# The first p moved ahead of the first k on SyncE's queue, and every operation in a newly searched order: a packed-attention and token-mixing kernel on one Trainium2 core

## The chip, the cores and the metric

The kernel runs on one core of a Trainium2 chip. The metric is the device time of one execution in microseconds. Before the change the median of three runs is 122.78 us (122.41 to 123.39). A measurement of this kernel can tell a difference of about one per cent from none.

## What is computed

All inputs are fp32; there are 8 batches (index b), 8 heads, 576 tokens, 64 channels a head and 32 packed queries a head (p).

```python
def sm_attn(qq, kk, vv):                       # softmax attention, scale 1/8
    s = scale * qq @ kk.T
    a = exp(s - max(s)); a = a / sum(a)
    return a @ vv
p_packed = sm_attn(p, k, v)                    # 32 x 64 for each batch and head
attn     = sm_attn(q, p_packed, p_packed)      # 576 x 64 for each batch and head
x = attn, heads side by side                   # 8 x 576 x 512
W = (x @ w_q) @ (x @ w_k).T / 8                # 576 x 576 for each batch
out = relu(W @ x) @ w_out                      # 8 x 576 x 512, fp32
```

## The kernel before

Nothing is scheduled by a compiler. The kernel defines about a hundred small operations, and a long string, `SCHEDULE`, lists every instance of them in the order in which they are recorded. Each engine works through its own instructions in exactly that order, so an instruction that waits holds up everything behind it on its engine, and engines wait for each other by semaphores only. An item reads `name@b`, then a letter and, after a colon, the PSUM banks: `kt0@1:3` is operation `kt0` of batch 1 into bank 3. The letter `s`, `v` or `g` puts a copy on ScalarE (ACT), VectorE (DVE) or GpSimd (POOL); `f` or `c` runs a matrix product on TensorE (PE) as one 128-column or as two 64-column matmuls.

What happens to a batch, with the lines under which the profile lists it:

- `LK LQ LV` (L148) load k, q, v of a batch by POOL's DMA queue, which converts to bf16 on the way. Eight of POOL's transfers can be under way; the issue of a further one first waits for the landing of the one eight places before it.
- `kt0 kt1`, `qt0 qt1` (L304) transpose k and q on PE; `ke0 ke1 qe0 qe1` copy the results from PSUM to SBUF (copies are L135 on ACT, L137, L139 and L141 on DVE).
- `s0` (L345) multiplies p by k, `nm0` (L355, DVE) takes the negative row maximum, `ex0 ex1` (L359, ACT) the exponentials and their sums, `rc1` the reciprocals, `rm` (L408, POOL) a masked copy of these.
- `xt0 xt1` (L376) transpose the weights, `xe0 xe1` copy them, `pv` (L421) multiplies by v, `pp` (L430) scales: this is p_packed. `pt pte` transpose it.
- `e0 e1 e2` (L470, L482) are the scores of q against p_packed; `mx0..2` and `sb0..2` (L498, L502, DVE) take and subtract maxima, `x0` (L531, ACT) is the exponential, `sm0` the sums (one reduction on DVE, L537, or a tree of five adds on POOL, L540 to L543), `rr0` the reciprocals, `ml0 ml1 ml2` (L551, DVE or POOL) the products that give the attention weights in three parts. `at0 at1` (L571, L574) transpose them, `ae0 ae1` copy.
- `pq wk wz wq g y m0 m1 m2` (L449, L628, L639, L660, L675, L683, L699, L714, L739) are the mixing products without ever forming x; `r00..r11 r2` apply the relu in the copy out of PSUM.
- `o0..o4` (L755) are the projections by `w_out`, `oe0..oe4` copy them, `st0..st2` and `sc0..sc3` (L786, L782, L772) store by SyncE's (SP's) DMA queue.

The batches overlap: while one is in its projections, the next ones are in their softmaxes and the loads run two to three batches ahead. Items `w1@..`, `w2@..` (L203) are one or two dummy products with a tile of zeros, which keep PE running where the order expects it to have nothing to do.

The first batch has a way of its own. Its k comes unconverted by SP's queue in two halves, `KA` and `KB` (L169, tile `k_f`); `cA0 cA1 cB0 cB1` convert them (tile `k_sb`), `kf0..kf3` transpose on PE (L257; `kf0`, `kf1` of the half of `KA`, `kf2`, `kf3` of that of `KB`), `kfe0..kfe3` copy. Its p comes fp32 by SP's queue (`PF`, L166, tile `p_f`); `pfc` converts it (tile `p_h`), `tp` transposes (L219), `lp` copies it into `pT_bd`. The p of the other batches comes by POOL's queue (`PB`, L179, tile `p_b`), is transposed by 32 matmuls `tr` (L233) and copied by `lq0`, `lq1`. The small weights are loaded by `cw0..cw3` (L278) and `wo0`, `wo1` (L287). `id` makes the identity on POOL.

The tiles of each name rotate through the buffers that `SLOTS` gives (six each for k, q and v, for example).

Of the kernel before, what the change touches and what calls it, by code (L numbers as in the profile page):

```python
# [21 lines left out]
    kt0@3:7 xe0@2s kt1@3:5 g@0f:2 LV@3 LK@5 rm@2 sb0@1 pv@2:3 LK@6 wqe@0s ke1@3v ke0@3s ge@0s y@0:5
    x0@1 pp@2 s0@3:0 ye@0s m0@0:45 r00@0s r01@0s nm0@3 m1@0:67 ex0@3 r11@0v w1@0c:3 qt1@2:3 qe1@2v
    pt@2f:5 pte@2v ex1@3 qt0@2:7 qe0@2v r10@0s w1@0f:3 sm0@1g rr0@1 ml1@1v ml0@1g ml2@1g LQ@5
    xt1@3c:0 xe1@3s LQ@4 LV@4 kt0@4:1 e0@2c:7 mx0@2 LK@7 xt0@3c:5 xe0@3v rc1@3 ke0@4s kt1@4:2 ke1@4s
    rm@3 e2@2:0 LQ@6 mx2@2 e1@2f:6 mx1@2 at0@1f:1 at1@1f:4 sb2@2 o1@0f:5 ae0@1s sb0@2 s0@4:0 sb1@2
    ae1@1s wk@1f:4 nm0@4 wq@1:7 wqe@1v oe1@0s x0@2 o0@0c:6 oe0@0v ex0@4 ex1@4 qt0@3:5 wz@1 o2@0f:7
    xt0@4f:6 wkx@1 wke@1s sm0@2v xe0@4v rr0@2 qe0@3s xt1@4f:0 g@1f:2 ge@1s pv@3:3 pp@3 y@1:5 ye@1s
    oe2@0s qt1@3:1 xe1@4v pt@3c:3 LV@5 m0@1:05 qe1@3v m1@1:46 m2@1f:7 ml1@2g ml0@2g pq@2:1 r00@1v
    pqe@2v pte@3s pq@3:2 e0@3f:3 r01@1s e2@3:0 pqe@3v e1@3f:5 r11@1s r2@1s r10@1s mx2@3 mx1@3 sb1@3  # L30
    sb2@3 ml2@2g LV@6 mx0@3 at0@2c:6 kt1@5:1 kt0@5:4 ae0@2s ke1@5s at1@2f:7 o2@1f:5 ae1@2s o3@0f:6
    wk@2f:7 wz@2 rc1@4 sb0@3 ke0@5v s0@5:0 oe2@1v wkx@2 x0@3 kt1@6:3 kt0@6:5 wke@2s oe3@0s wq@2:6
    nm0@5 ke0@6s ex1@5 ke1@6v wqe@2v o1@1f:7 g@2f:3 ex0@5 ge@2s qt1@5:4 qt0@5:6 st1@0 oe1@1v qt0@4:7
    y@2:2 sm0@3g rr0@3 qe1@5v qt1@4:0 ye@2v m1@2:23 qe0@4v r11@2v ml0@3g rm@4 qe0@5s o4@1f:6 qe1@4s
    rc1@5 r10@2s pv@4:4 m0@2:01 ml1@3g oe4@1s r00@2s ml2@3v at0@3f:7 xt1@5f:2 pp@4 ae0@3s r01@2v
    pt@4f:3 rm@5 LQ@7 pte@4v at1@3f:4 ae1@3s xt0@5f:0 xe1@5v e0@4f:3 mx0@4 LV@7 xe0@5s e1@4f:7 mx1@4
    o3@2f:5 oe3@2s sb0@4 wk@3f:2 e2@4:1 mx2@4 wz@3 wkx@3 wke@3s wq@3:6 wqe@3s kt0@7:0 s0@6:3 sb2@4
    o2@2c:1 sb1@4 kt1@7:6 ke0@7s x0@4 o0@1f:2 pq@4:0 nm0@6 ex1@6 ke1@7v ex0@6 sm0@4g oe2@2v oe0@1s
    qt1@6:6 pqe@4v qt0@6:1 qe0@6s qe1@6v rc1@6 s0@7:3 g@3f:2 ge@3s nm0@7 rm@6 pv@5:6 y@3:0 pp@5
    o3@1f:2 ye@3v rr0@4 ex1@7 ex0@7 pt@5f:7 xt0@6f:6 pte@5v xt1@6f:0 xe0@6v ml1@4g st0@1 m2@3f:1  # L40
    r2@3s e1@5f:7 e0@5f:3 ml0@4g oe3@1s m1@3:64 r10@3s xe1@6v pv@6:0 ml2@4g pq@5:2 o1@2c:5 pqe@5s
    mx1@5 mx0@5 pp@6 r11@3s sb1@5 e2@5:2 pt@6c:0 pte@6s at0@4f:1 mx2@5 rc1@7 ae0@4s at1@4f:4 sb0@5
    xt0@7f:7 rm@7 sb2@5 xe0@7s e1@6f:0 ae1@4v xt1@7f:3 xe1@7v st0@0 o4@3f:2 mx1@6 sb1@6 x0@5 sm0@5g
    wk@4f:3 m0@3:76 r01@3v wq@4:1 oe4@3s e2@6:4 wz@4 wke@4v wkx@4 oe1@2s r00@3s e0@6c:0 mx0@6 st2@3
    wqe@4s o0@2c:2 oe0@2s qt1@7:6 g@4c:1 o0@3c:5 st1@2 qe1@7s sb0@6 ge@4v y@4:2 mx2@6 pv@7:0 st2@1
    rr0@5 ml0@5g sb2@6 pp@7 qt0@7:7 ye@4s m1@4:43 oe0@3s ml2@5v m0@4:01 x0@6 pt@7c:5 pq@6:2 qe0@7v
    o2@3c:6 at0@5c:7 st1@1 pte@7s ml1@5g st0@2 r00@4v pqe@6v e0@7c:0 e2@7:5 r11@4s at1@5c:3 pq@7:2
    r01@4v ae0@5v mx0@7 r10@4s o1@4c:1 e1@7c:7 sm0@6g oe2@3s ae1@5s mx2@7 wk@5c:3 sb0@7 o0@4c:4 wz@5
    mx1@7 sb2@7 wq@5:0 o3@3c:5 sb1@7 oe1@4s rr0@6 wkx@5 wqe@5v o1@3c:7 wke@5s oe0@4s st0@4 x0@7
    ml1@6g pqe@7v oe3@3s st1@3 g@5c:3 ge@5s o2@4c:2 oe1@3s y@5:3 ml0@6g ye@5s ml2@6v sm0@7v rr0@7  # L50
# [782 lines left out]
```

## Time and profile before

| | before |
|---|---|
| median of 3 runs | 122.78 us (122.41 to 123.39) |
| the profiled execution | 122.19 us, its span 120.4 us |
| busy: PE, PE's weight loads, DVE, ACT, POOL | 105.2, 69.2, 94.0, 88.6, 59.5 us |
| moved by POOL's queue | 14.49 MB in 13,920 packets |
| moved by SP's queue | 10.68 MB in 3,984 packets |
| granted TensorE clock | 1.00 throughout |

The span goes from the first to the last instruction on the core; the 1.8 us between it and the execution's own time lie around it. Busy time on PE is that of matmuls whose ends are modelled. A row of the timeline gives start, length, engine, line, operation, output and inputs, and in brackets how long the engine had been idle before it and what ended that. A row of a group by form gives count, busy time and mean in ns, and the idle time before. A row of a transfer gives the time from issue to landing.

### The profile page before, as it was taken

How to read it: one execution, taken by the hardware profiler on the slowest of the kernel's cores; microseconds unless marked ns; L12 is line 12 of the kernel's file. 1: busy time of each engine (PE TensorE's matmuls, PEld its weight loads, DVE VectorE, ACT ScalarE, POOL GpSimd, SP SyncE). 2: the span in 40 equal slices, each digit the busy share in tenths (PEclk: the TensorE clock that was granted, in tenths of full speed). 3: DMA queues.
4: the chain of work that ended last, by engine and by line, in shares of the span. 5: the costliest groups of instructions: out<-in, count | busy, mean ns of one | idle time of the engine just before them, and what ended most of it. 6: DMA issues, size and time to landing. Idle time of an engine off the chain costs nothing.

```text
span 120.4 us, 4740 instructions
## 1 busy us (share of the span) xinstructions
PE 105.2 (87%) x2041; PEld 69.2 (57%) x2055; DVE 94.0 (78%) x192; ACT 88.6 (74%) x159; POOL 59.5 (49%) x85
## 2 busy tenths in 40 slices
PE   6955677879998999999999989999999969999980
...
DMA  3999999999999999999999999994940484045793
GB/s 51 372 207 204 207 205 208 194 208 208 208 208 204 209 206 210 207 209 207 209 289 208 208 213 203 290 251 155 393 178 5 195 328 169 14 186 201 310 383 145
DMA packets 17925, 25.47 MB, mean 212 GB/s; under 512 B 2160, under 2 KB 14448, under 8 KB 17904
## 3 DMA queue, kind: packets, MB, share of 16 engines
q0 software_dynamic: 13920, 14.49, 71.6%
q1 hardware_dynamic: 3984, 10.68, 23.5%
...
## 4 chain that ended last, share of the span: by engine, by line
PE 45%; ACT 16%; DVE 14%; DMA 14%; POOL 4%; issue 3%; SPq 1%; DVEq 0%; POOLq 0%
PE psum L755 16%; DMA out_dram<-o_sb 8%; DMA p_f<-in_p_dram 6%; PE psum L304 5%; ACT e1T L359 4%; ACT e L531 4%; DVE mx L498 3%; PE psum L571 3%; DVE e L502 3%; PE psum L421 3%; ACT kT L135 3%; PE psum L714 2%; PE psum L660 2%; PE psum L345 2%; PE psum L203 2%
## 5 line engine op out<-in xcount | busy, mean ns | idle before, releaser
L755 PE MATMUL psum<-w_out,r 128*64 128x512 bf16 (+1 forms) x184 | 30.7, 380 | 0.7 <-issue 0.5
L551 POOL TENSOR_TENSOR a<-e,rr 128x512 bf16<-128x512 f32 (+1 forms) x16 | 16.0, 1019 | 10.4 <-DVE rr L547 7.3
L135 ACT ACTIVATE o_sb<-psum 128x512 f32<-128x512 f32 x25 | 14.9, 602 | 6.0 <-PE psum L755 4.1
L755 PEld LDWEIGHTS <-r 128*64 128x64 bf16 (+1 forms) x192 | 12.4, 106 | 11.1 <-issue 1.3
L359 ACT ACTIVATE e1T<-psum,nmax 128x576 bf16<-128x576 f32 x16 | 11.7, 739 | 5.0 <-DVE nmax L355 4.9
L135 ACT ACTIVATE kT<-psum 128x1280 bf16<-128x1280 bf16 (+2 forms) x10 | 10.4, 1043 | 5.1 <-DVE mx L498 3.3
L498 DVE TENSOR_REDUCE mx<-psum 128x16 f32<-128x512 f32 (+1 forms) x24 | 12.7, 550 | 0.9 <-PE psum L470 0.8
L540 POOL TENSOR_TENSOR rt<-e 128x576 f32<-128x576 f32 x5 | 7.1, 1417 | 12.4 <-ACT e L531 12.3
L502 DVE TENSOR_TENSOR e<-psum,mx 128x512 f32<-128x512 f32 (+1 forms) x24 | 12.6, 548 | 0.1
L355 DVE TENSOR_REDUCE nmax<-psum 128x2 f32<-128x1152 f32 x8 | 10.8, 1355 | 2.0 <-PE psum L345 1.8
L203 PE MATMUL psum<-zero 128*64 128x512 bf16 (+1 forms) x45 | 10.7, 477 | 1.4 <-DVE zero L182 1.2
L135 ACT ACTIVATE r<-psum 128x512 bf16<-128x512 f32 x19 | 10.8, 600 | 1.0 <-PE psum L714 1.0
L304 PE MATMUL psum<-ident,q_sb 128*64 128x128 bf16 x288 | 10.6, 220 | 0.6 <-DVE r L137 0.3
L531 ACT ACTIVATE e<-e 128x1152 f32<-128x1152 f32 x8 | 9.4, 1169 | 1.2 <-DVE e L502 1.2
L304 PEld LDWEIGHTS <-q_sb 128*64 128x64 bf16 x288 | 9.1, 110 | 1.7 <-issue 0.5
L137 DVE TENSOR_SCALAR r<-psum 128x512 bf16<-128x512 f32 x13 | 8.6, 684 | 0.9 <-PE psum L714 0.8
L304 PE MATMUL psum<-ident,k_sb 128*64 128x128 bf16 x252 | 8.6, 219 | 0.0
L135 ACT ACTIVATE qT<-psum 128x1280 bf16<-128x1280 bf16 (+1 forms) x7 | 8.1, 1152 | 0.6 <-PE psum L304 0.6
L542 POOL TENSOR_TENSOR rt<-rt 128x288 f32<-128x288 f32 (+2 forms) x15 | 7.9, 528 | 1.2
L304 PEld LDWEIGHTS <-k_sb 128*64 128x64 bf16 x252 | 7.8, 110 | 0.9 <-issue 0.2
L135 ACT ACTIVATE a2T<-psum 128x768 bf16<-128x768 bf16 (+1 forms) x12 | 8.1, 702 | 0.2
L408 POOL TENSOR_TENSOR rm<-mask,rrec 128x256 f32<-128x256 f32 x8 | 5.0, 627 | 6.2 <-DVE rrec L369 6.2
...
## 6 DMA issues: line engine op xcount, KB each, us to landing
...
q_sb<-in_q_dram POOLq DMA_DIRECT2D x8, 576.0 KB, 14.8
v_sb<-in_v_dram POOLq DMA_DIRECT2D x8, 576.0 KB, 17.2
k_sb<-in_k_dram POOLq DMA_DIRECT2D x7, 576.0 KB, 17.3
k_f<-in_k_dram SPq DMA_DIRECT2D x2, 576.0 KB, 4.5
out_dram<-ox SPq DMA_DIRECT2D x4, 256.0 KB, 2.7
out_dram<-o_sb SPq DMA_DIRECT2D x4, 256.0 KB, 2.5
w_out<-in_moe_w_out_dram POOLq DMA_DIRECT2D x2, 256.0 KB, 11.9
```

Source lines behind the costliest of these rows:

```text
L135: nc.scalar.activation(dst, src, func, scale=scale)
L137: nc.vector.tensor_scalar(dst, src, 0.0, None, op0=MAX)
L203: nc.tensor.matmul(bank(ks[0])[r], zero[:, r], zero, start=True, stop=True, skip_group_check=True,)
L304: nc.tensor.transpose(tp[64 * g2:64 * g2 + 64, gp, :, 64 * (j - j0):64 * (j - j0) + 64], S_[b][src][:, gp + 2 * g2, order[j]], ident,)
L355: nc.vector.tensor_reduce(tile("nmax", [P, 2], fp32, b), S_[b]["s1"], axis=AX, op=MAX, negate=True)
L359: nc.scalar.activation(tile("e1T", [P, NJ, 2, 64], bf16, b)[:, :, h2], S_[b]["s1"][:, h2].rearrange("a (j s) -> a j s", j=NJ), EXP, bias=S ...
L498: nc.vector.tensor_reduce(units(i, tile("mx", [P, NU, 1], fp32, b)), S_[b]["e", i], axis=AX, op=MAX)
L502: nc.vector.tensor_tensor(units(i, tile("e2", [P, NU, L], fp32, b)), S_[b]["e", i], m.to_broadcast((P, m.shape[1], L)), op=SUB,)
L531: nc.scalar.activation(e, e, EXP, scale=scale)
L542: nc.gpsimd.tensor_tensor(t[:, :, 0:w], t[:, :, 0:w], t[:, :, w:2 * w], op=ADD)
L551: (nc.gpsimd if on == "g" else nc.vector).tensor_tensor(tile("a2", [P, NU, L], bf16, b)[:, r], S_[b]["e2"][:, r], S_[b]["rr"][:, r].to_bro ...
L755: nc.tensor.matmul(ps[r], src[:, i, r], w_out[:, i, :], start=(i == 0), stop=(i == 3),)
```

## The change

`PF` stands in front of both k halves on SP's queue, the half of `KB` comes before that of `KA`, `PB` is the first transfer on POOL's queue, and the items of the string stand in a new order, with new banks, new letters for some copies and products, and the dummy products elsewhere. Every operation on every batch is still there once; only the number of dummy products differs (30 before, 28 after). The functions and `SLOTS` are unchanged. The k, q and v loads after the first batch keep their order among each other.

```diff
 SCHEDULE = """
-    w1@0c:1 KA@0 LQ@0 cA0@0s w1@0c:0 cA1@0v w1@0f:1 w2@0c:1 w1@0c:0 KB@0 PB@0 w2@0c:1 w1@0c:0 LV@0
-    cw3@0 id@0 kf0@0:1 cB1@0v cB0@0v LK@1 w1@0f:5 PF@0 pfc@0v LQ@1 kfe0@0s kf1@0:4 kfe1@0v kf2@0:0
-    kfe2@0s kf3@0:2 w1@0c:1 tp@0:5 kfe3@0v lp@0v s0@0:0 nm0@0 qt1@0:3 LK@2 w1@0f:5 ex1@0 ex0@0
-    tr@0:57 w1@0c:6 qe1@0s lq0@0v rc1@0 xt0@0f:2 xe0@0v w1@0c:1 xt1@0c:5 cw2@0 xe1@0v qt0@0:1 qe0@0v
-    lq1@0s w1@0c:0 cw0@0 cw1@0 pv@0:4 rm@0 pp@0 pt@0c:5 pte@0v w1@0f:2 w1@0f:6 e1@0c:5 mx1@0 e0@0f:2
-    e2@0:6 w1@0c:4 LV@1 mx0@0 mx2@0 kt1@1:0 ke1@1s sb0@0 LK@3 kt0@1:3 ke0@1v sb1@0 sb2@0 LV@2 s0@1:0
-    nm0@1 x0@0 sm0@0v rr0@0 w1@0c:4 qt1@1:6 qe1@1s w1@0c:3 w1@0f:3 ex0@1 qt0@1:4 w1@0f:3 LQ@2
-    kt1@2:5 ml0@0v kt0@2:7 ml1@0g ex1@1 rc1@1 xt1@1f:0 at0@0f:2 ke1@2s xt0@1f:1 xe0@1s ke0@2v ml2@0v
-    s0@2:5 at1@0f:3 rm@1 ae0@0v qe0@1v LK@4 nm0@2 pq@0:2 xe1@1s pv@1:0 ae1@0s w1@0c:4 pqe@0s wk@0f:2
...
+    w1@0c:2 PF@0 w1@0c:0 PB@0 LQ@0 LV@0 id@0 w1@0f:1 KB@0 cB1@0v w1@0c:0 w2@0f:2 pfc@0s w1@0f:1
+    w1@0f:5 LK@1 LQ@1 w2@0f:1 KA@0 cA1@0v tp@0:0 w1@0c:2 w2@0f:1 kf3@0:5 cB0@0s kf2@0:2 w1@0c:1 LK@2
+    tr@0:34 lp@0s kfe2@0v w1@0f:1 kf1@0:6 cA0@0s kf0@0:1 w1@0c:2 kfe1@0v kfe0@0v kfe3@0s s0@0:0
+    nm0@0 cw0@0 w1@0f:5 w1@0f:5 lq0@0s cw2@0 ex0@0 lq1@0v w1@0c:6 w1@0f:6 w1@0c:5 w1@0c:3 ex1@0
+    rc1@0 cw3@0 qt0@0:6 xt1@0f:0 rm@0 xt0@0f:1 xe0@0v qt1@0:2 LV@1 xe1@0s qe1@0v pv@0:0 pp@0 w1@0f:3
+    qe0@0s pt@0c:2 pte@0v e0@0c:0 mx0@0 sb0@0 w1@0c:6 kt0@1:5 e2@0:7 mx2@0 sb2@0 kt1@1:2 cw1@0
+    ke0@1s e1@0f:6 mx1@0 sb1@0 ke1@1s w1@0f:0 x0@0 LK@3 LV@2 s0@1:3 nm0@1 ex1@1 ex0@1 qt1@1:6
+    w1@0f:2 LQ@2 sm0@0v rr0@0 rc1@1 rm@1 w2@0c:2 w1@0c:1 kt1@2:0 kt0@2:2 xt0@1c:3 ke0@2v qt0@1:5
+    xt1@1f:4 ml2@0g qe0@1v ke1@2s s0@2:0 ml1@0g ml0@0g nm0@2 xe0@1s LK@4 w1@0f:3 xe1@1s pv@1:3 pp@1
+    at1@0f:5 ae1@0v qe1@1s ex0@2 ex1@2 at0@0f:6 ae0@0s pt@1c:3 wo0@0 pte@1v pq@0:4 pqe@0s wo1@0
...
```

77 lines of the change are left out of this document (38 added, 39 removed).

## The prediction

> **What bounds the kernel now.** I read the page first (busy shares, slices), then the busy time by stretch, the timeline of the first 30 us, the transfers, and last the chain of work that ended last. The page:
>
> ```profile
> PE 105.2 (87%) x2041; PEld 69.2 (57%) x2055; DVE 94.0 (78%) x192; ACT 88.6 (74%) x159; POOL 59.5 (49%) x85
> PE   6955677879998999999999989999999969999980
> DMA  3999999999999999999999999994940484045793
> ```
>
> TensorE (PE) is the busiest engine, and its slices are full from about the ninth on; the transfers are full from the second slice to the twenty-sixth. Cut by stage (columns: length, then busy us and instructions of PE, PE's weight loads, DVE, ACT, POOL; clock; transfers):
>
> ```profile
> 0.00:10.00 10.00, 6.52 (x57) 2.52 (x57) 4.67 (x17) 3.43 (x4) 6.86 (x15) 1.00 0.88 209
> 10.00:25.00 15.00, 11.09 (x283) 8.45 (x288) 11.99 (x24) 8.00 (x15) 4.46 (x7) 1.00 1.28 204
> 25.00:45.00 20.00, 18.24 (x407) 13.29 (x405) 18.86 (x38) 18.56 (x34) 16.27 (x22) 1.00 1.22 207
> 45.00:95.00 50.00, 48.80 (x1047) 34.28 (x1051) 46.20 (x97) 43.51 (x80) 30.42 (x42) 1.00 0.98 211
> 95.00:116.00 21.00, 19.70 (x257) 10.46 (x258) 12.32 (x21) 14.53 (x29) 1.46 (x1) 1.00 0.57 225
> ```
>
> From 45 to 116 us PE stands still for only 50.0 - 48.8 = 1.2 and 21.0 - 19.7 = 1.3 us: there the end is PE's own work. The ramp before 45 us is different. From 25 to 45 us DVE (18.9) and ACT (18.6 of 20) are fuller than PE, which idles 1.8 us and spends some of its busy time on dummy matmuls with `zero`, which the order puts where PE has nothing to do:
>
> ```profile
> 25.00:45.00 20.00, 1.57 (x7) 0.52 (x8) 1.00 1.22 207
> ```
>
> So 1.8 + 1.6 = 3.3 us of PE are lost there, and more before 25 us, where the first batch goes through alone. At the end nothing is to be had: the last 35 projection matmuls run back to back (last row of the fence on loads below). The change has to win or lose in the ramp.
>
> **The head (first scores, `s0@0`).** Timeline rows of the start, then transfer rows: queue 1 (SP's) from 2.7 to 5.2 us, where queue 0 (POOL's) moved nothing, and from 5.6 to 8.8 us, where both did (packets, MB, share of the 16 engines); then the times from issue to landing.
>
> ```profile
> 0.74 0.96 SPq L169 DMA_DIRECT2D k_f<-in_k_dram  x2
> 1.19 4.25 PE L203 MATMUL psum<-zero 128*64 128x512 bf16 x17 [1.19 <-DVE zero L182]
> 1.25 0.93 POOL L148 DMA_DIRECT2D q_sb<-in_q_dram  x1 [0.81 <-POOLq L817]
> 1.74 0.47 SPq L166 DMA_DIRECT2D p_f<-in_p_dram  x1
> 2.17 0.55 POOL L179 DMA_DIRECT2D p_b<-in_p_dram  x1
> 4.76 0.74 ACT L135 ACTIVATE k_sb<-k_f 128x640 bf16<-128x640 f32 x1 [2.74 <-DMA k_f<-in_k_dram]
> 6.27 1.03 DVE L141 CAST k_sb<-k_f 128x512 bf16<-128x512 f32 x2 [1.08 <-DMA k_f<-in_k_dram]
> 7.36 0.69 PE L257 MATMUL psum<-ident,k_sb 128*64 128x128 bf16 x18 [0.67 <-DVE k_sb L141]
> 9.17 0.23 DVE L141 CAST p_h<-p_f 128x128 bf16<-128x128 f32 x1 [1.86 <-DMA p_f<-in_p_dram]
> 10.47 0.68 PE L345 MATMUL psum<-kT,pT_bd 128*64 128x512 bf16 x8 [0.79 <-DVE pT_bd L139]
> 11.97 1.08 PE L233 MATMUL psum<-ident,p_b 128*64 128x128 bf16 x32 [0.25 <-issue]
> ```
>
> ```profile
> q1 hardware_dynamic: 438, 0.97, 100.1%
> ...
> q1 hardware_dynamic: 282, 0.08, 17.2%
> ...
> p_b<-in_p_dram POOLq DMA_DIRECT2D x1, 256.0 KB, 8.4
> p_f<-in_p_dram SPq DMA_DIRECT2D x1, 64.0 KB, 7.4
> ```
>
> Before: the two k halves are there at 4.76 and 6.27, p_f, third on SP's queue, only at 1.74 + 7.4 = 9.1. PE has all k transposes done at 8.05 and waits; `p_h` at 9.17, the transpose of p, `lp`, scores at 10.47.
>
> After: p_f is first. A packet of it takes 0.172 x 3.2 us x 16 / 282 = 31 ns, so its 256 packets are 0.5 us on 16 engines; alone on the engines it should land by 3 to 4 us, and that wait is gone. The halves start 0.5 us later (one issue slot, 0.96 / 2), and their 512 packets, at 438 per 2.5 us, then reach to about 6.2 instead of 5.7 us: landings 5.3 and 6.8. Next in line are two things that did not stand in the way before:
>
> - PE's queue. Ahead of the p transpose stand 10 dummy units (a unit is one 128-wide matmul or a pair of 64-wide ones); 9 units took 4.25 us at the start, so 10 take 4.7 and end at 5.9. Three more units, the transposes of one k half (0.69 for 18), one unit, then `tr`, the 32 transposes of p_b (1.08), which used to run at 11.97 under the row maximum, now stand ahead of the second half's transposes. With 0.4 for a unit by itself (between the 0.47 above and the 0.22 below) the sum is 5.9 + 0.2 + 3 x 0.4 + 0.69 + 0.4 + 1.08 + 0.4 + 0.69 + a last copy of 0.5 = 11.1; at the 7.72 / 35 = 0.22 us of the back-to-back projections at the end it is 10.2, and 9.9 if the last of the ten already run so.
> - p_b, now first on POOL's queue. It landed 10.57, behind q_sb at about 9.4; so it takes 1.2 us of queue 0, which starts near 5.2: 6.4 alone, 7.9 if it shares with k. `tr` can start at about 7.5 to 8, so this does not end last unless queue 0 starts later.
>
> `s0@0` comes at 9.9 to 11.1; I take 10.3, near the lower sum because the units do overlap: a gain of 0.2 (0.6 gained to 0.6 lost), where the removed wait alone would have given 1.9 (scores at 8.05 and a copy of 0.5).
>
> The Trainium skill ("DMA: Bandwidth & Descriptors", Queues, rings and completion order) says that an engine takes turns between queues packet by packet. The rows agree for p_f: from 5.6 to 8.8 us 282 packets of SP's queue went out with POOL's at work beside them. By that rule the second half of k, still under way when p_b begins, would wait behind p_b's longer packets, an estimate of up to 1.2 us more, and `s0@0` would be at 11.1 or later, the upper end above.
>
> **From the first scores to batch 1.** Two copies that DVE did one after the other (`xe0@0`, `xe1@0`) go to DVE and ACT side by side, and the max and subtract steps of batch 0 are no longer broken by a k copy (`ke0@1` goes to ACT): about 0.4 us earlier each. Against it, `kt0@1` now stands ahead of `e2@0` and `e1@0` on PE and waits for the second batch's k, whose place in the load order is unchanged. I take 0.5 us in PE's favour by the scores of batch 1 (0 to 1.0).
>
> **POOL's queue.** It issues the loads, and with 8 in flight each issue waits for the landing 8 places back.
>
> ```profile
> 20.69 0.74 POOL L148 DMA_DIRECT2D q_sb<-in_q_dram  x1 [2.09 <-DMA q_sb<-in_q_dram]
> 25.15 0.69 DVE L551 TENSOR_TENSOR a<-e,rr 128x512 bf16<-128x512 f32 x1
> 25.28 1.48 POOL L551 TENSOR_TENSOR a<-e,rr 128x512 bf16<-128x512 f32 x1 [3.85 <-DVE rr L547]
> ...
> 27.57 0.33 PE psum L571 x4
> 42.86 0.61 PE psum L345 x8
> ```
>
> `LQ@2` waited for `LQ@1` (20.69). Since one small weight load moved back, it now waits for `LK@2`, at 23.5 by the next fence, and is issued by 24.3; behind it on POOL stand `rm@1` and now all three multiplies `ml2@0 ml1@0 ml0@0`, of which DVE had two (0.69 for the large one; POOL's large one is 1.16 on the mean). Estimate: the multiplies' input 0.5 us before the 25.15 of the row, at 24.6, `rm@1` to 25.4, then 0.4 + 1.16 + 1.16: done at 28.1, where POOL's large one was done at 25.28 + 1.48 = 26.8 before, and batch 0's second transposes ran at 27.57. The rest of batch 0 (`wk`, `wq`, `g`, `y`) comes 1 to 2 us later. The order covers this: PE has other work ahead of `at0@0` that used to follow it (`s0@2`, 0.61 as in the last row, `pv@1`, 0.53 as in the fence on loads, `xt0@1` and `at1@0`, about 0.3 each): 1.7 us. So 0, and up to +1.5 if that cover is late.
>
> The skill ("SBUF — State Buffer", SBUF: two separate sides) says that DVE's fast modes and POOL exclude each other from a shared port. The 1.48 us of the multiply beside DVE's, against 1.16, agrees; at 1.48 each the chain would end 0.6 later, inside the bound just given.
>
> **Who copies what.** Rows by form:
>
> ```profile
> L551 POOL TENSOR_TENSOR a<-e,rr 128x512 bf16<-128x512 f32 x13 | 15.0, 1163 | 10.4 <-DVE rr L547 7.3 <-PE psum L714 1.9 <-DVE e L502 0.6
> L135 ACT ACTIVATE a2T<-psum 128x768 bf16<-128x768 bf16 x6 | 4.9, 809 | 0.1
> L135 ACT ACTIVATE r<-psum 128x512 bf16<-128x512 f32 x19 | 10.8, 600 | 1.0 <-PE psum L714 1.0
> L141 DVE COPY a2T<-psum 128x768 bf16<-128x768 bf16 x2 | 1.1, 554 | 0.0
> L137 DVE TENSOR_SCALAR r<-psum 128x512 bf16<-128x512 f32 x13 | 8.6, 684 | 0.9 <-PE psum L714 0.8
> ```
>
> bf16 copies are cheaper on DVE (0.55 against 0.81), fp32 ones on ACT (0.60 against 0.68), and the new order sorts them so. Over the whole kernel, with each form's mean, ACT does 0.7 and DVE 1.6 us less, POOL 1.1 more. More telling is the ramp: up to `s0@4` (42.86 in the POOL fence) 17 ops worth 10.2 us leave DVE and 12 worth 7.7 come (ACT: 8.2 out, 10.6 in; POOL: 2.5 in, 1.0 out). DVE, the fuller one, has 2.5 us less before that point. PE cannot gain more than the 3.3 us it loses there; that copies were what it lacked holds for some of them, and others are latency. I take 1.0 (0 to 2.5). The dummy units in that stretch also fall, from five behind `pv@1` to one.
>
> **What the loads allow.** Issue, time to landing, first use; and the end of PE:
>
> ```profile
> 6.22 0.79 POOL L148 DMA_DIRECT2D k_sb<-in_k_dram  x1
> 63.95 0.75 POOL L148 DMA_DIRECT2D v_sb<-in_v_dram  x1
> ...
> k_sb<-in_k_dram POOLq DMA_DIRECT2D x1, 576.0 KB, 17.3
> v_sb<-in_v_dram POOLq DMA_DIRECT2D x1, 576.0 KB, 18.8
> ...
> 85.42 0.53 PE psum L421 x36
> 108.25 7.72 PE psum L755 x35
> ```
>
> `LV@7` lands at 63.95 + 18.8 = 82.75 and is read at 85.42; behind it PE has 30.6 us to its last projection. The order of the k, q and v loads is the same in both kernels and queue 0 never runs dry, so this landing hardly moves: 2.7 us is the most that PE can gain, plus what queue 0 starts earlier (up to about 1 us).
>
> **Sum**, against the profiled execution's 122.19 (span 120.4 and 1.8 around it): head -0.2, batch 0 to 1 -0.5, POOL 0, copies -1.0, tail 0: 120.5. That execution lies 0.6 under the runs' median of 122.78, so the forecast is 121.1.
>
> **The rivals.**
> - No change (within 1%, about 1.2 us, which is what a measurement of this kernel can tell): the loads pin the ramp. For: even 60 us later `LV@7` has only 2.7 us of slack, so a faster first batch may only wait for loads. Against: PE idles in 25 to 45 us for more than loads. Time: head 0, batch 0 to 1 at 0, copies -0.3: 122.5.
> - Slower: POOL's multiplies decide. If the cover ahead of `at0@0` is not ready (it needs `LV@1` and ACT, which now has 2.4 us more before `s0@4`), batch 0's last multiply at 28.1 against 26.8 leaves 1.3 us of PE idle, up to 1.6 with each multiply at 1.48 and `rm@1` late; `tr` ahead of k with `s0@0` at 11.1 adds up to 0.6. Point from which it decides: `at0@0` after 28.5 us with PE idle over 1 us just before it. Time: 122.8 + 1.3 to 2.2, I put 124.4.
> - The change does not deliver p early: if p_f's small packets still land after 6 us, `s0@0` slips with `lp` to 11 or later; inside the two cases above, as its price is 0.5.
>
> **How the numbers follow.** Faster by the sum 0.43, no change 0.32, slower 0.25. The predicted time is 121.1; its own range is 119.7 (2.7 of slack and 0.4 of scatter below the median) to 121.5. The range for 8 in 10 takes in no change and about half of the slower case: 119.7 to 124.3.
>
> **What would show it.** Right: p cast before 5 us; `s0@0` between 9.9 and 11.1; PE's idle plus dummy time from 25 to 45 us down from 3.3 to about 2; `LV@7` still landing at 82 to 83 and read within 2 us; the last 35 projections still back to back. Wrong: `tr` waiting for p_b after 8.5; POOL's last multiply of batch 0 after 28.5 with PE idle; new idle time of over 1 us between 45 and 95 us, which I put at none without having followed each wait there.

## The result and the profile after

The change makes the kernel slower by about one per cent: 124.02 us (median of 8 runs, 123.26 to 124.34) against 123.08 us (8 runs of the kernel before on the same chip, 122.41 to 123.49), ratio 1.0105 with a 95% interval of 1.0065 to 1.0144. The 0.94 us are at the edge of what a measurement of this kernel can tell, and less than the 1.2 us up to which the prediction spoke of no change, but the interval lies wholly above 1. The profiled execution of the changed kernel has a span of 122.2 us, that of the kernel before 120.4. The ratios of the experiments below are taken against runs of the kernel before made beside them (median 122.64 us for e1 to e4, 122.16 for e5 to e8, 122.06 for e9 to e12) and leave out runs in a slower state of the chip, so they are not the quotients of the medians given.

The changed kernel has 31 dummy units, not 28, as was said of the change; the kernel before has 30.

From the page of the changed kernel, then the busy time by stretch, then the dummy products from 25 to 45 us (the same views as in the prediction):

```profile
PE 107.7 (88%) x2022; PEld 68.7 (56%) x2022; DVE 95.3 (78%) x186; ACT 87.8 (72%) x164; POOL 59.3 (49%) x86
PE   6986677989989898999999999999989979999920
DMA  3999999999999999999999999980954070555981
```

```profile
0.00:10.00 10.00, 7.66 (x79) 3.34 (x79) 3.52 (x13) 3.48 (x6) 7.00 (x15) 1.00 0.86 205
10.00:25.00 15.00, 12.01 (x261) 7.92 (x255) 11.49 (x21) 9.31 (x18) 4.24 (x6) 1.00 1.26 205
25.00:45.00 20.00, 18.36 (x418) 13.12 (x418) 18.47 (x36) 18.44 (x34) 17.29 (x24) 1.00 1.23 207
45.00:95.00 50.00, 48.67 (x1036) 33.55 (x1034) 45.62 (x92) 43.84 (x83) 29.27 (x41) 1.00 1.00 219
95.00:116.00 21.00, 20.16 (x247) 10.53 (x243) 15.53 (x27) 12.13 (x27) 1.50 (x2) 1.00 0.48 194
```

```profile
25.00:45.00 20.00, 0.80 (x3) 0.21 (x3) 1.00 1.23 207
```

Read alone, this looks like the forecast: from 25 to 45 us idle and dummy time of PE fell from 3.3 to 1.64 + 0.80 = 2.4 us. But a fixed window does not show the same work in both kernels. So a second measure is used below, the lag: PE's products are added up in their order, each kind at one fixed duration, dummies left out, and the times at which two executions reach the same sum are compared. The zero is the profiled execution of before; "at 48" means at the work that it had reached at 48 us. Between kernels with different orders the lag depends on the durations chosen: with other fixed durations the changed order's values at 42 us come out 0.5 to 0.7 higher, those at 48, 82 and 116 within 0.4.

The head, timeline rows of the changed kernel, then what the two queues moved from 4.4 to 8.7 us (packets, MB, share of the 16 engines):

```profile
2.73 0.31 ACT L135 ACTIVATE p_h<-p_f 128x128 bf16<-128x128 f32 x1 [0.72 <-DMA p_f<-in_p_dram]
5.39 0.43 DVE L141 CAST k_sb<-k_f 128x512 bf16<-128x512 f32 x1 [1.53 <-DMA k_f<-in_k_dram]
7.24 1.06 PE L233 MATMUL psum<-ident,p_b 128*64 128x128 bf16 x32
9.28 0.43 DVE L141 CAST k_sb<-k_f 128x512 bf16<-128x512 f32 x1 [3.46 <-DMA k_f<-in_k_dram]
9.77 0.78 PE L257 MATMUL psum<-ident,k_sb 128*64 128x128 bf16 x18 [1.15 <-DVE k_sb L141]
11.13 0.68 PE L345 MATMUL psum<-kT,pT_bd 128*64 128x512 bf16 x8 [0.37 <-DVE kT L141]
```

```profile
q0 software_dynamic: 371, 0.52, 68.4%
q1 hardware_dynamic: 316, 0.66, 42.7%
```

p is cast at 2.73 instead of 9.17. The second half of k, though, is read at 9.28 instead of 6.27, and the first scores start at 11.13 instead of 10.47. SP's queue sent 316 packets in these 4.3 us, 73 per us, where alone it had sent 438 in 2.5 us, 175 per us. The Trainium skill ("DMA: Bandwidth & Descriptors", Queues, rings and completion order) says that each engine takes turns between queues packet by packet. The trace agrees in part: 371 and 316 packets go out side by side over the 4.3 us, but not evenly. From 5.0 to 5.6 us SP's queue sent only 3 packets against 58 of POOL's, and from 6.0 to 7.5 us 194 against 67. Why it paused is open, and the 73 per us includes the pause.

Executions of one kernel differ, so two more of each kernel were profiled (e13 to e16 below). The profiled executions differ by more than the runs: those of before took 121.50 to 122.19 us, below all eight runs above, those of the changed kernel 123.38 to 124.40, among its runs. So the traces explain a difference of about 1.4 us, the runs show 0.94. The table puts all executions together with the experiments; all its columns are worked out from the traces, in us. "Read" is the start of the first copy of the second half of k, "between" the time from the end of the last copy out of PSUM to the end of the span, and the last column the start of the 16th and last 16 KB packet of instructions.

| execution | read | lag at 16 | at 42 | at 48 | at 82 | at 87 | at 116 | last copy ends | span | between | instr. |
|---|---|---|---|---|---|---|---|---|---|---|---|
| before | 6.27 | 0 | 0 | 0 | 0 | 0 | 0 | 116.65 | 120.38 | 3.72 | 106.8 |
| e13, before | 6.53 | -0.7 | -0.2 | -0.2 | -0.2 | -0.2 | -0.2 | 116.47 | 120.20 | 3.73 | 106.6 |
| e16, before | 6.26 | -0.7 | -0.5 | -0.6 | -0.6 | -0.7 | -0.7 | 115.98 | 119.70 | 3.73 | 106.2 |
| after | 9.28 | +0.3 | 0.0 | +1.3 | +0.9 | +0.3 | +0.8 | 117.50 | 122.21 | 4.71 | 114.7 |
| e14, after | 9.68 | +0.7 | +0.4 | +1.7 | +1.5 | +1.0 | +1.3 | 117.92 | 122.63 | 4.71 | 115.2 |
| e15, after | 9.64 | +0.7 | +0.4 | +1.7 | +1.2 | +0.7 | +1.2 | 117.88 | 121.61 | 3.73 | 122.2 |
| e1 | 9.02 | +2.7 | +2.7 | +2.7 | +2.7 | +2.1 | +2.5 | 119.15 | 122.88 | 3.73 | 109.2 |
| e2 | 9.52 | +3.2 | +3.2 | +3.2 | +3.2 | +2.6 | +3.0 | 119.66 | 123.38 | 3.72 | 109.8 |
| e3 | 9.48 | +0.7 | +0.4 | +1.7 | +1.2 | +0.7 | +1.2 | 117.89 | 121.68 | 3.79 | 122.0 |
| e4 | 9.82 | +0.9 | +0.5 | +1.8 | +1.4 | +0.9 | +1.4 | 118.04 | 121.78 | 3.74 | 112.9 |
| e5 | 6.22 | -1.5 | -0.9 | -1.0 | -0.1 | -0.2 | -0.2 | 116.44 | 120.16 | 3.72 | 106.6 |
| e6 | 7.01 | +0.9 | +0.9 | +0.9 | +0.9 | +1.0 | +1.0 | 117.66 | 121.39 | 3.72 | 107.8 |
| e7 | 7.18 | -0.8 | +0.1 | +1.4 | +1.0 | +0.5 | +1.0 | 117.64 | 121.38 | 3.74 | 122.4 |
| e8 | 7.56 | -0.1 | -0.1 | +1.2 | +0.8 | +0.2 | +0.8 | 117.41 | 121.65 | 4.24 | 113.0 |
| e9 | 9.08 | +1.1 | +1.1 | +1.1 | +1.1 | +1.0 | +1.0 | 117.64 | 121.37 | 3.73 | 107.5 |
| e10 | 9.61 | +0.7 | +0.3 | +1.6 | +1.2 | +0.7 | +0.6 | 117.24 | 121.02 | 3.79 | 121.4 |
| e17, as e10 | 10.02 | +1.1 | +0.9 | +2.2 | +1.8 | +1.2 | +1.2 | 117.83 | 121.56 | 3.74 | 122.6 |
| e18, as e10 | 9.67 | +0.7 | +0.4 | +1.7 | +1.2 | +0.7 | +0.6 | 117.29 | 122.00 | 4.70 | 114.5 |
| e11 | 9.81 | +1.4 | +1.0 | +2.2 | +1.7 | +1.2 | +1.1 | 117.79 | 121.81 | 4.02 | 112.7 |
| e12 | 6.81 | -0.8 | 0.0 | +1.2 | +0.7 | +0.2 | +0.1 | 116.76 | 120.76 | 4.00 | 111.5 |

On the means of three executions each, the changed kernel's last copy ends 117.77 - 116.37 = 1.4 us later, and its tail is 0.0 or 1.0 us longer. By the lag, the 1.4 us arise like this (difference of the means): +1.0 at 16 us, +0.5 at 42 (up to +1.1 with other durations), +1.8 at 48, +1.5 at 82, +1.4 at 116.

### The profile page after: what moved, and what is told of

It reads as the page before. It is cut to its first block, busy times and chain, and to the rows that moved or that the text cites. A ratio compares the mean times of both kernels' runs of the same rounds, so it can differ in the third digit from the quotient of the medians.

```text
span 122.2 us, 4677 instructions
## 1 busy us (share of the span) xinstructions
PE 107.7 (88%) x2022; PEld 68.7 (56%) x2022; DVE 95.3 (78%) x186; ACT 87.8 (72%) x164; POOL 59.3 (49%) x86
## 4 chain that ended last, share of the span: by engine, by line
PE 48%; DVE 23%; ACT 7%; POOL 6%; DMA 6%; issue 4%; SPq 1%; DVEq 0%; ACTq 0%; POOLq 0%
PE psum L755 18%; PE psum L304 8%; DMA k_f<-in_k_dram 6%; DVE nmax L355 3%; DVE mx L498 3%; PE psum L345 3%; ACT e1T L359 2%; DVE e L502 2%; PE psum L470 2%; PE psum L714 2%; PE psum L376 2%; DVE rs L537 2%; DVE qT L141 2%; PE psum L660 2%; PE psum L421 2%
## 5 line engine op out<-in xcount | busy, mean ns | idle before, releaser
L755 PE MATMUL psum<-w_out,r 128*64 128x512 bf16 (+1 forms) x192 | 31.8, 381 | 0.5 <-DVE e L502 0.5
L135 ACT ACTIVATE o_sb<-psum 128x512 f32<-128x512 f32 x24 | 14.3, 605 | 6.9 <-PE psum L755 6.6
L551 POOL TENSOR_TENSOR a<-e,rr 128x512 bf16<-128x512 f32 (+1 forms) x17 | 15.6, 936 | 6.5 <-DVE rr L547 5.4
L203 PE MATMUL psum<-zero 128*64 128x512 bf16 (+1 forms) x45 | 11.5, 449 | 1.5 <-DVE zero L182 1.2
L135 ACT ACTIVATE r<-psum 128x512 bf16<-128x512 f32 x22 | 11.7, 602 | 1.1 <-PE psum L714 0.9
L141 DVE COPY qT<-psum 128x1280 bf16<-128x1280 bf16 (+1 forms) x12 | 8.9, 754 | 1.4 <-PE psum L304 1.2
L141 DVE COPY o_sb<-psum 128x512 f32<-128x512 f32 x8 | 5.5, 688 | 3.5 <-PE psum L755 3.5
L148 POOL DMA_DIRECT2D q_sb<-in_q_dram x8 | 6.1, 764 | 3.6 <-DMA k_sb<-in_k_dram 2.7
## 6 DMA issues: line engine op xcount, KB each, us to landing
q_sb<-in_q_dram POOLq DMA_DIRECT2D x8, 576.0 KB, 14.3
```

Source lines behind the costliest of these rows:

```text
L135: nc.scalar.activation(dst, src, func, scale=scale)
L141: nc.vector.tensor_copy(dst, src)
L203: nc.tensor.matmul(bank(ks[0])[r], zero[:, r], zero, start=True, stop=True, skip_group_check=True,)
L551: (nc.gpsimd if on == "g" else nc.vector).tensor_tensor(tile("a2", [P, NU, L], bf16, b)[:, r], S_[b]["e2"][:, r], S_[b]["rr"][:, r].to_bro ...
L755: nc.tensor.matmul(ps[r], src[:, i, r], w_out[:, i, :], start=(i == 0), stop=(i == 3),)
```

## The experiments

### What moving p does by itself

e1, the kernel before with that one move:

```diff
-    w1@0c:1 KA@0 LQ@0 ...      ... LK@1 w1@0f:5 PF@0 pfc@0v ...
+    w1@0c:1 PF@0 KA@0 LQ@0 ... ... LK@1 w1@0f:5 pfc@0v ...
```

> The kernel before with one part of the change alone: the transfer of p_f stands ahead of both halves of k on SP's queue, nothing else is moved. Theory A (the second half of k, slowed by POOL's queue, holds the first scores of the changed kernel, and the early p itself is good): here POOL's queue starts as before, at about 5.3 us, so p_f lands by 3, the halves of k by 5.7 and 6.5, p is cast at once when VectorE comes to it, and s0 of batch 0 starts at 8.6 to 9.2 instead of 10.5. If time won at the start reaches the end, the ratio is 0.985 to 0.99 (121.2 to 121.8 us against 123.0). Theory B (the loads pin the middle of the kernel, so nothing won or lost in the first 12 us reaches the end): s0 as early, ratio 0.997 to 1.003.

Measured: 124.55 us, ratio 1.0189 (1.0144 to 1.0234). Timeline rows, then the windows (columns as above, the clock third from the end), then the group of q's transposes from 9.5 to 16 us:

```profile
9.02 0.83 DVE L141 CAST k_sb<-k_f 128x512 bf16<-128x512 f32 x2 [3.25 <-DMA k_f<-in_k_dram]
9.90 1.17 PE L257 MATMUL psum<-ident,k_sb 128*64 128x128 bf16 x18 [2.57 <-DVE k_sb L141]
12.27 1.17 PE L345 MATMUL psum<-kT,pT_bd 128*64 128x512 bf16 x8 [0.55 <-DVE pT_bd L139]
```

```profile
9.00:12.00 3.00, 1.82 (x21) 1.15 (x21) 1.95 (x7) 0.70 (x1) 1.18 (x2) 0.62 1.18 208
12.00:16.00 4.00, 3.26 (x48) 2.68 (x51) 1.57 (x2) 1.04 (x3) 0.05 (x1) 0.50 1.27 204
```

```profile
L304 PE MATMUL psum<-ident,q_sb 128*64 128x128 bf16 x20 | 1.3, 314 | 0.0
```

Both theories fail here. A expected POOL's queue to start as before and the second half by 6.5; it is read at 9.02, and the scores start at 12.27. B expected that nothing of the head reaches the end; the lag is 2.7 us from 16 to 82 us and still 2.5 at the last projection. And there is a part that neither named: while PE idled 2.57 us for k, its clock fell to 0.50 and stayed there until about 16.5 us; a transpose took 314 ns instead of 219. The column does not always show this: two of e1's six runs have a mean granted clock of 0.998 or more and, at 124.35 and 124.93 us, are no shorter.

e2 added the other move of the head, p_b first on POOL's queue:

```diff
-    w1@0c:1 PF@0 KA@0 LQ@0 ... KB@0 PB@0 w2@0c:1 ...
+    w1@0c:1 PF@0 KA@0 PB@0 LQ@0 ... KB@0 w2@0c:1 ...
```

> The kernel before with p_f ahead of k on SP's queue and p_b as the first transfer of POOL's queue, the rest as before: the two moves of the head that the changed kernel makes, without its new order. Theory A: POOL's packets start a microsecond earlier, at about 4.3 us, share the engines with the second half of k, and this half (here that of KB) lands at about 9.2 instead of 6.2; s0 of batch 0 starts at 11 or later. If the head reaches the end, ratio 1.003 to 1.01; theory B: 0.997 to 1.003. If the second half of k lands by 7, theory A's account of the late half (POOL's queue) is wrong.

Measured: 125.61 us, ratio 1.0263 (1.0205 to 1.0320). The second half of k lands at 9.5, 0.5 us later than in e1 and near theory A's 9.2, but its ratio (1.003 to 1.01) was missed by far: the median is 1.1 us longer than e1's. Not all of that is the landing. The transposes of q took 314 ns up to 16.5 us here as well, while the clock column read 1.00 throughout.

e3 undid p_b's place in the changed kernel:

```diff
-    ... PB@0 LQ@0 LV@0 id@0 ...   ... tr@0:34 lp@0s ...   ... s0@0:0 nm0@0 ...
+    ... LQ@0 PB@0 LV@0 id@0 ...   ... lp@0s ...           ... s0@0:0 tr@0:34 nm0@0 ...
```

> The changed kernel with the load of q of batch 0 ahead of p_b on POOL's queue, as before the change, and the 32 transposes of p_b behind s0 of batch 0 on TensorE so that they hold up nothing. Theory A: POOL's packets start at 5.3, the second half of k lands at about 6.5 instead of 9.2, s0 of batch 0 starts at 9.0 to 9.7 instead of 11.1; if that reaches the end the time falls by 1 to 1.6 us against the changed kernel (ratio to before 0.997 to 1.003). Theory B: the head is as much shorter but the end stands where it stood, ratio 1.008 to 1.014.

Measured: 123.9 us, ratio 1.0144 (1.0088 to 1.0201). The second half is read at 9.48, not at 6.5, and the end comes no earlier: both theories fail. So it does not matter which of POOL's transfers goes first. What is left is that any of them is on the engines while k is under way, and e6 below tries that.

### The clock

e9 is e1 with dummies in the two gaps (one line more in the list, so its line numbers are one higher):

```diff
-    ... cw3@0 id@0 kf0@0:1 ...            ... kf1@0:4 kfe1@0v kf2@0:0 ...
+    ... cw3@0 id@0 w2@0c:1 kf0@0:1 ...    ... kf1@0:4 w9@0f:5 kfe1@0v kf2@0:0 ...
```

> The kernel of e1 (p_f first on SP's queue, otherwise before) with 11 more dummy products, two ahead of the first transposes of k and nine between those of its first and its second half, where TensorE sat idle for 0.65 and 2.57 us. In e1 the granted clock was 0.50 from about 9.5 to 16.5 us and a transpose took 314 ns instead of 219. Theory W (0.9 of the 2.7 us that e1 lies behind in the middle are the clock that TensorE loses by idling): the transposes after 9.5 us take 219 ns, the lag behind the kernel before is about 1.8 instead of 2.7 us from 16 us on, ratio 1.010 to 1.014 (e1: 1.019). If the clock falls all the same, or the lag stays at 2.7 with the clock at 1.00, theory W is wrong.

Measured: 123.19 us, ratio 1.0083 (1.0058 to 1.0107). A timeline row, a window and a group:

```profile
11.59 0.68 PE L346 MATMUL psum<-kT,pT_bd 128*64 128x512 bf16 x8 [0.55 <-DVE pT_bd L140]
```

```profile
12.00:16.00 4.00, 2.74 (x67) 2.11 (x64) 3.02 (x7) 2.22 (x5) 0.54 (x2) 1.00 1.28 206
```

```profile
L305 PE MATMUL psum<-ident,q_sb 128*64 128x128 bf16 x20 | 0.7, 219 | 0.0
```

k is read as late as in e1 (9.08), the clock stays at 1.00, and the lag is 1.1 instead of 2.7 us. Theory W holds and was too small: the clock is 1.6 of e1's 2.7 us by the lag, and 1.4 us by the medians (124.55 against 123.19). The Trainium skill ("TensorE: Matmul & The Clock Gate", What's actually happening) says that TensorE halves its clock after a window of about 3.4 us without work, and doubles it after as long a one with work. The half clock agrees; here a shorter gap, 2.57 us without work, behind 0.65 us and a few transposes, was enough.

### When POOL's queue starts

The next four hold POOL's first transfer back from 1.25 to 2.99 us: POOL zeroes `pT_bd` (1.80 us) and makes the identity before it. e5 does that to the kernel before, e6 to the kernel of e1:

```diff
-    nc.vector.memset(pT_bd, 0.0)
+    nc.gpsimd.memset(pT_bd, 0.0)
...
-    ... KA@0 LQ@0 ...        ... cw3@0 id@0 kf0@0:1 ...
+    ... KA@0 id@0 LQ@0 ...   ... cw3@0 kf0@0:1 ...
```

> The kernel before with POOL's first transfer held back by 1.5 to 2.5 us: POOL, not VectorE, zeroes pT_bd, and makes the identity ahead of its first transfer; p_f stays behind both halves of k. What e1 suggests (theory A2: what lands when is decided by which of the two queues has packets on the engines first; theory P: a shift of the first scores goes through to the end one for one, because TensorE has no slack behind it): the halves of k land at 4.7 and 5.9 to 6.2, p_f, no longer mixed with q's packets, lands at 6.5 to 7 instead of 9.1, s0 of batch 0 starts at 8.6 to 9.2 instead of 10.5, ratio 0.985 to 0.99. Theory B (the loads pin the middle): q, v and the later loads land up to 1 us later or as before, ratio 0.998 to 1.01.

Measured: 121.50 us, ratio 0.9959 (0.9934 to 0.9985): 0.4% under the kernel before, less than the one per cent that a measurement is said to tell, though the interval lies below 1. Timeline rows:

```profile
7.16 0.21 DVE L141 CAST p_h<-p_f 128x128 bf16<-128x128 f32 x1
9.00 0.68 PE L345 MATMUL psum<-kT,pT_bd 128*64 128x512 bf16 x8 [0.64 <-DVE pT_bd L139]
62.36 0.70 PE L421 MATMUL psum<-v_sb,e 64*64 64x128 bf16 x36 [0.81 <-DMA v_sb<-in_v_dram]
```

p_f, still third on SP's queue, is there by 7.16, and the scores start at 9.00. So the wait for p that the change set out to remove goes without moving p at all. POOL's first packet hardly moved, though: 5.46 us, against 5.27 to 5.41 in the three executions of before. p_f's 256 packets went out between 5.22 and 5.91 us, where in the executions of before they took until 7.99 to 8.73. That POOL's packets make the difference is shown by e6, not by e5 alone. The edit also takes the zeroing of `pT_bd` off DVE, which was waiting for k at that time; that part was not tried by itself. The gain of 1.5 us then shrinks: 1.0 us is left at 48 us, and at 62.36 PE waits 0.81 us for v of batch 4; behind that 0.1 is left. Here theory B is right: what is won at the start is lost to the loads.

> The kernel of e1 (p_f first on SP's queue, otherwise before) with POOL's first transfer held back in the same way. Theory A2: POOL's packets come after the last of k's, the second half of k lands at 6.3 to 6.8 instead of 9.0, s0 of batch 0 starts at 8.8 to 9.3 instead of 12.3, the granted clock stays at 1.00 from 9 to 18 us (0.50 in e1); with theory P the time is 3 us below e1, ratio 0.985 to 0.99. If the second half of k lands after 8 all the same, not POOL's packets but the later issue or p's small packets slow it.

Measured: 122.9 us, ratio 1.0054 (1.0027 to 1.0081). Timeline rows, and q's transposes from 6 to 14 us:

```profile
7.01 0.96 DVE L141 CAST k_sb<-k_f 128x512 bf16<-128x512 f32 x2 [0.91 <-DMA k_f<-in_k_dram]
10.48 1.17 PE L345 MATMUL psum<-kT,pT_bd 128*64 128x512 bf16 x8 [0.63 <-DVE pT_bd L139]
```

```profile
L304 PE MATMUL psum<-ident,q_sb 128*64 128x128 bf16 x20 | 1.3, 312 | 0.0
```

POOL's first packet comes at 6.22 us, against 4.52 in e1, and the second half is read at 7.01 instead of 9.02: POOL's packets were the cause. The expectation for the scores (8.8 to 9.3) and the ratio (0.985 to 0.99) were missed. The scores start at 10.48: PE is at half speed (312 ns a transpose, up to 14.2 us), and the lag is 0.9 us where e5 has -1.5. This is not a fall of the clock: every execution starts at half speed, and this one reaches full speed only at 14.3 us, e5 with the same dummies at 7.2. The likely reason is that the first half of k is read at 5.51, after the dummies have run out (PE idled 0.81 us before its first transposes); unlike e1's, this gap was not filled in an experiment.

e7 holds POOL back in the changed kernel, with e3's place of `tr`:

```diff
-    nc.vector.memset(pT_bd, 0.0)
+    nc.gpsimd.memset(pT_bd, 0.0)
...
-    ... PB@0 LQ@0 LV@0 id@0 ...   ... tr@0:34 lp@0s ...   ... s0@0:0 nm0@0 ...
+    ... id@0 PB@0 LQ@0 LV@0 ...   ... lp@0s ...           ... s0@0:0 tr@0:34 nm0@0 ...
```

> The changed kernel with POOL's first transfer held back in the same way and the 32 transposes of p_b behind s0 of batch 0 on TensorE. Theory A2: the second half of k lands at 6.3 to 6.8 instead of 9.2, s0 of batch 0 starts at 8.7 to 9.3 instead of 11.1; theory P: the end comes 1.5 to 2.2 us earlier, ratio to before 0.993 to 0.999. Theory B: ratio 1.008 to 1.014 as the changed kernel.

Measured: 123.92 us, ratio 1.0168 (1.0134 to 1.0201). The head does what was expected (POOL's first packet at 6.04, scores at 9.79, lag -0.8 at 16 us); at 42 us the lag is +0.1, so nothing of it is left, and at 48 us it is +1.4, as in the changed kernel. The early head buys nothing, and the faster time that theory P expected did not come.

### The end

e4 reorders the last 8 us of the changed kernel, e8 that of e7:

```diff
-    ... o3@6f:3 o2@6f:7 r01@7v st1@5 r10@7s r11@7s o1@6f:2 oe2@6v o0@6f:5 st0@5 ... st0@6 ... st2@7 ...
+    ... o0@6f:3 o1@6f:7 r01@7v st1@5 r10@7s r11@7s o4@7f:0 oe0@6v o3@6f:6 st0@5 ... st0@6 o2@6f:5 oe4@7v st2@7 ...
```

> The changed kernel with the projections, copies and stores of the last 8 us in another order, the first two rows of blocks of batch 6 and the shared block of batch 7 first, so that the stores st0 of batch 6 and st2 of batch 7 are issued at about 111.5 and 112.8 instead of 113.2 and 116.1; same engines for as many copies. Theory C (0.9 of the 1.8 us lost are stores that queue up behind each other at the end): the span ends 3.8 us after the last copy instead of 4.7, time -0.6 to -1.0 us, ratio to before 1.002 to 1.006. Rival: the stores only share the same rate, what is stored last ends when it did: ratio 1.009 to 1.012.

> The kernel of e7 with the order of the last 8 us of e4 (stores st0 of batch 6 and st2 of batch 7 earlier). Theory C (0.9 us of the loss are stores that queue up at the end): 0.6 to 1.0 us below e7, ratio to before 0.986 to 0.993; if the stores are at their rate anyway, as e7 within 0.3 us.

Measured: e4 123.85 us, ratio 1.0127 (1.0077 to 1.0176); e8 123.29 us, ratio 1.0114 (1.0072 to 1.0156), 0.6 us under e7, with intervals that overlap. Theory C fails as the sole reason: the order of the stores alone does not decide. e3 and e7 keep the changed order and end 3.79 and 3.74 us after the last copy; e8, reordered, ends 4.24 after it and e4 3.74.

Four more executions of the two kernels, unchanged, show what goes with it:

> The kernel before, unchanged, a second profiled execution, to see what differs between executions of one kernel: if its stages are its own, the second half of k lands at 6.2 (plus or minus 0.2), the span ends 3.7 us after the last copy, TensorE's curve lies within 0.2 us of the first execution's except for stretches at a lower granted clock.

> The changed kernel, unchanged, a second profiled execution. Theory A (the late half of k): the second half of k lands at 9.2 to 9.8 again, as in the four other executions with this head. Theory C (stores queue up at the end by their order): the span ends 4.5 to 4.9 us after the last copy as in the first; against it, three experiments with the same order of stores ended 3.74 to 3.79 after it, so 3.7 to 3.8 if the first was its own.

> As the run before it, a third execution: the same numbers; what differs between the three is the spread of this kernel and no effect of the change.

> As the first of these four, a third execution of the kernel before: the same numbers.

Transfers from 113.5 to 117 us (packets, MB, share; then issue to landing), in e14 and in e15, the same kernel:

```profile
q1 hardware_dynamic: 389, 1.16, 85.0%
q8 instruction: 1, 0.02, 1.7%
...
out_dram<-o_sb SPq DMA_DIRECT2D x1, 512.0 KB, 4.6
out_dram<-o_sb SPq DMA_DIRECT2D x2, 256.0 KB, 4.1
```

```profile
q1 hardware_dynamic: 452, 1.29, 92.9%
...
out_dram<-o_sb SPq DMA_DIRECT2D x1, 512.0 KB, 3.0
out_dram<-o_sb SPq DMA_DIRECT2D x2, 256.0 KB, 2.6
```

e14 ends 4.71 us after its last copy, as theory C had it, but e15, the same kernel, 3.73: the order of the stores does not settle it. The executions of before, e13 and e16, were 0.2 to 0.7 us ahead of the first execution of before, more than the 0.2 expected. In e14 one 16 KB packet of instructions, 0.93 us long, falls among the last stores (115.2 us), and every store behind it lands about 1.5 us later after its issue. In e15 it comes at 122.2, after the end. e17 and e18 tried that rule on the kernel of e10, which had the widest spread:

> The kernel of e10 (the changed kernel with the products of batch 5 back on POOL), a second profiled execution. Its profiled execution lay 0.6 us ahead of the changed kernel's after 98 us, yet its twelve times went from 122.8 to 125.1 and their median was that of the changed kernel. Theory I (a 16 KB transfer of instructions that falls among the last stores costs an execution about 1 us, in the changed order in some executions, before the change never): where that transfer starts at 113 to 116 us the span ends 4.5 to 4.9 us after the last copy, where it starts after 120 us, 3.7 to 3.8. The other part of the spread would be the head: second half of k at 9.2 to 9.9, TensorE at half clock for some microseconds or not.

> A third execution of the kernel of e10: as the run before it. If the span ends 4.5 us after the last copy without that transfer, or 3.7 us with it at 113 to 116 us, theory I is wrong.

Measured: e17 without it 3.74 us, e18 with it (114.5) 4.70 us. Over the eight executions with the changed order of stores, the three with the packet at 114.5 to 115.2 end 4.70 to 4.71 us after the last copy, the five without it 3.73 to 3.79. With the end reordered (e4, e8, e11, e12) it comes at 111.5 to 113.0, and they end 3.74 to 4.24 after it. In the order of before it comes at 106 to 107 in all three executions, when SP's queue carries little:

```profile
q1 hardware_dynamic: 103, 0.42, 34.8%
q8 instruction: 1, 0.02, 3.4%
```

That was 105 to 108 us in the first execution of before. So the long end goes with the packet in every case, and e17 and e18 bore the rule out, but no run moved the packet by itself. Which engine's instructions these are, and what decides between 115 and 122 us, no run shows.

### The middle

e10 gives the products of batch 5 back to POOL:

```diff
-    ... ml2@5g m0@4:01 ...               ... ml0@5v e1@7c:2 ...   ... mx1@7 ml1@5g ...
+    ... ml1@5g ml0@5g ml2@5v m0@4:01 ... ... e1@7c:2 ...          ... mx1@7 ...
```

> The changed kernel with the products of batch 5 as before the change: ml0 and ml1 on POOL, the small ml2 on VectorE (the change put ml0 on VectorE, 1.60 us of its time while it is the last to finish, between 88 and 98 us). Theory D (a copy or product that the change puts on VectorE late in the kernel costs its length): x0 and sm0 of batch 7 1.0 to 1.5 us earlier, the second half of the stretch loses 0.5 to 1.0 us less, ratio to before 1.002 to 1.006. If the projections before 100 us take the room, no more than 0.3 us: 1.008 to 1.012.

Measured: 123.96 us, ratio 1.0141 (1.0106 to 1.0176). First the changed kernel, then e10:

```profile
88.40 1.60 DVE L551 TENSOR_TENSOR a<-e,rr 128x512 bf16<-128x512 f32 x1
90.06 0.41 PE L571 MATMUL psum<-ident,a 128*64 128x128 bf16 x8 [0.57 <-DVE a L551]
```

```profile
87.32 0.86 DVE L551 TENSOR_TENSOR a<-e,rr 128x128 bf16<-128x128 f32 x1
```

The large product took DVE 1.60 us beside a busy POOL, and PE waited for it; the small one that replaces it takes 0.86. From 87 to 116 us the lag grows by 0.3 to 0.5 us in the three executions of the changed kernel, in e3 and in e4, and by -0.1, 0.0 and -0.1 in the three of e10, so theory D holds in the traces, at about 0.5 us. In the times it does not show: the ratio is no better than e3's or e4's. The two further executions (e17, e18) show what varies by as much, the head (0.7 to 1.1 us at 16) and the packet of instructions (3.7 or 4.7 us at the end); how often each falls which way in the twelve times is not known.

e11 adds a repair at 42 to 48 us and the end of e4, e12 also the head of e7:

```diff
-    ... wq@1:0 wqe@1v rm@3 LQ@5 LQ@4 wkx@1 LV@4 qt0@3:7 pqe@2s x0@2 wke@1s LK@7 ...
+    ... wq@1:0 rm@3 LQ@5 LQ@4 LV@4 qt0@3:7 pqe@2s wke@1s wkx@1 x0@2 wqe@1s LK@7 ...
```

> The changed kernel with three repairs of its order, the head left alone: the products of batch 5 as in e10; in batch 1 the copy wke ahead of wkx and of x0 of batch 2, and wqe on ScalarE behind x0 (ScalarE sat idle 0.94 us there, VectorE was the last); the last 8 us as in e4. Theory C plus D: -0.7 from the end, -0.5 to -1.0 from 88 to 98, -0.3 to -0.6 from 42 to 50 us, together 1.5 to 2.3 us off the changed kernel, ratio 0.991 to 0.998. If the loads pin the stretch up to 62 us here too, the repair at 42 to 50 gives nothing: 0.996 to 1.001.

> The kernel of e11 with the head of e7 (POOL's first transfer held back, the transposes of p_b behind s0 of batch 0). If the head's gain (1.3 us at s0 of batch 0) reached the end it would be 1 us below e11; as e5 lost its 1.5 us to waits for loads by 66 us, the expectation is 0 to 0.4 us below e11, ratio 0.988 to 0.996.

Measured: e11 123.27 us, ratio 1.0084 (1.0050 to 1.0119); e12 122.61 us, ratio 1.0033 (1.0007 to 1.0059), the changed order's best, and still not faster than before. Both are slower than was expected. In e11 PE's clock fell to 0.50 from 12.2 to 15.6 us, after a gap of 1.87 us; in e10, with the same head and a gap of 1.72, it did not. The window from 41 to 50 us in the kernel before and in the changed one, then what PE waited for in it, in the changed kernel and in e11 (us in total, times, longest):

```profile
41.00:50.00 9.00, 8.84 (x164) 5.79 (x161) 8.81 (x18) 8.33 (x16) 7.06 (x11) 1.00 1.21 207
41.00:50.00 9.00, 8.05 (x159) 5.03 (x155) 7.95 (x15) 7.75 (x16) 6.32 (x9) 1.00 1.21 207
```

```profile
PE psum L755 <- DVE e L502: 0.5, 1, 0.5
PE psum L683 <- ACT wk L135: 0.3, 1, 0.3
```

```profile
PE psum L755 <- DVE e L502: 0.5, 1, 0.5
PE psum L675 <- ACT wqT L135: 0.3, 1, 0.3
```

PE idles 0.95 us there instead of 0.16. The repair only swapped one wait for another: the lag grows by 1.2 us from 42 to 48 in e11 and e12, against 1.3 in the changed kernel. This loss, 0.8 us by idle time and 1.3 by the lag, is located, in waits for DVE and ACT around the projections of batch 0 and `g@1`, but not undone; which of the moved operations makes it stays open.

## Why the prediction was wrong

The forecast was 121.1 us and faster; the result is 124.02 and slower. By its steps:

- **The head**, -0.2 forecast. The step that failed is "landings 5.3 and 6.8": the first half was right (5.39), the second was read at 9.28 to 9.68. The prediction gave k's packets the speed that they have alone, although it had POOL's queue start at 5.2 with k under way until 6.2; that queue started at 4.33 to 4.95. The sentence that rests on the Trainium skill put the sharing at up to 1.2 us, and the second half came 2.5 to 2.9 later than forecast. e6 shows that POOL's packets cause it. The scores came at 11.13, the upper end of its bounds, and that this nearly fits is luck: the sum reached 11.1 by PE's own queue, while PE in fact stood still 1.15 us for the copy of the late half. By the lag the head costs 0.3 to 0.7 us against the profiled execution of before, and 1.0 on the means, because in that one execution p was cast at 9.17 and in the two others at 8.48 and 8.46: a part of the wait that the change was to remove belonged to that execution.
- **"The removed wait alone would have given 1.9."** e1 removed it alone and lost 1.9 us (124.55 against 122.64): the late k took the place of the late p, and PE's clock fell while it waited.
- **Batch 0 to 1**, -0.5: the lag falls by 0.3 us from 16 to 42 us in all three executions of the changed kernel, but with other durations the change lies between -0.9 and +0.1. A gain of 0.5 is neither shown nor ruled out.
- **POOL's queue**, 0 with up to +1.5: the transposes `at0@0` ran at 28.70, after the 28.5 named as the point from which the slower rival decides, but PE was not idle before them and the lag stayed flat. The cover held, and the rival's mechanism did not decide.
- **Copies**, -1.0: failed. DVE's relief is there (33.5 against 35.5 us busy up to 45 us, where 2.5 less was forecast up to `s0@4`), but it did not shorten anything: 0.8 to 1.3 us are lost from 41 to 50, and e10 shows a further 0.5 from 87 on, from the large product of batch 5 put on DVE. The prediction had put new idle time after 45 us at none, and said that it had not followed the waits there.
- **"2.7 us is the most that PE can gain"**: failed. `LV@7` lands at 82.9 and is read at 85.93, as forecast, but it is not the load that binds. In e5 the gain was gone at v of batch 4, at 62 us; 0.2 us were left at the end, and the times say 0.5 (ratio 0.9959). The rival "no change" had the mechanism right, and its price for a gain; for a loss there is no such brake, as e1, e6 and e9 show by lags that reach the end whole or nearly so.
- **Tail**, 0: the last projections are back to back as forecast, but in three of eight executions the stores behind them take 1.0 us longer.

By size, on the means: at 16 us the lag is +1.0 where -0.2 was forecast, and at 48 us +1.8 where -1.7 was. So 1.2 us of the error lie in the head and 2.3 between 16 and 48 us, where the copies were to give their gain. The cause of the first is shown; of the second the place is shown, and which moved operation makes it stays open. The second weighs more at the end: e7 takes the head's loss away and is as late as the changed kernel (lag +1.0 at 116 us), though the same step from e11 to e12 gained 0.7 us by the medians.
